# Attention scores: both single score tiles of a pair copied by VectorE and exponentiated in one instruction, a group's normalization placed ahead of P-V

## The chip, the core and the metric

The kernel runs on one core of one Trainium2 chip. A core has a matrix engine (TensorE, "PE" in the profile, with its weight loads as "PEld"), three engines for elementwise work (VectorE or "DVE", ScalarE or "ACT", GpSimd or "POOL"), and SyncE ("SP"), which here only issues transfers. Each engine works through its own queue in order; semaphores hold an instruction until what it needs is done. Matmuls write to PSUM, eight banks of 128 x 512 float32; everything else lies in SBUF or in the chip's main memory.

The metric is the device time of one execution in microseconds (us). The kernel before took 1995.16 us, the median of three runs (1995.09 to 1995.32).

## The reference

Two layers, each of them attention and a gated feed-forward block, over one sequence of S = 2048 tokens with D = 448 features, all in float32:

```python
def _A_ref(x, wq, wk, wv, wo):          # H = 16 heads, Dh = 28
    q = (x @ wq).reshape(B, S, H, Dh).transpose(0, 2, 1, 3)
    k, v = x @ wk, x @ wv               # one key and value head for all
    scores = einsum("bhqd,bkd->bhqk", q, k) * Dh ** -0.5
    o = einsum("bhqk,bkd->bhqd", softmax(scores), v)
    return o.transpose(0, 2, 1, 3).reshape(B, S, H * Dh) @ wo

def _B_ref(x, w_gate, w_up, w_down):    # F = 1792
    return (silu(x @ w_gate) * (x @ w_up)) @ w_down

x = x + _A_ref(layernorm(x)); x = x + _B_ref(layernorm(x))   # layer 0
x = x + _A_ref(layernorm(x)); x = x + _B_ref(layernorm(x))   # layer 1
```

The change is in the attention: scores, exponential, product with the values (P-V below), and the division by the sum of the exponentials.

## The kernel before

A layer runs projections (`finish`), then the score stage (`scores`), then the feed-forward block (`rest`). Float32 products outside P-V are split into a high and a low part and added up from three matmuls.

**The score stage** works by groups. A group is 512 query tokens and four heads; the list `GR` has 16 of them (4 blocks of tokens, index `c`, times 4 sets of heads, index `g`). For each group the 2048 keys pass in 16 tiles of 128. So the loop over `n` has 256 steps in a layer; `i, kt = divmod(n, NT)` gives the group and the key tile, and `d, odd = divmod(n, 2)` the pair of key tiles.

`step(n)` computes one key tile's scores for four heads: twelve matmuls (L595), three for each head, where the four heads use the four quarters of the array's rows. Heads 0 to 2 go into `three`, a PSUM tile of three banks; there are two of these, for even and odd tiles. Head 3 goes into a single bank, `one`. The single banks are number 6 and 7, by the function `single`: pair d uses bank 6 + d % 2 for its even tile and the other one for its odd tile. The exponentials go to SBUF, into `pt` (heads 0 to 2, three buffers, taken in turn from tile to tile) and `pt1` (head 3, three buffers). On ScalarE's queue a pair of tiles is four instructions: for the even tile the exponential of the single bank, straight from PSUM (L607), then that of the three banks (L608); for the odd tile that of the three banks (L602), then that of the single one (L605). For the odd tile VectorE first copies the single bank to SBUF, into `raw` (L604; one buffer), and L605 reads the copy.

`pv(d)` multiplies a pair's exponentials by the values (L638): eight matmuls with 32 columns of weights each, first the four heads of the even tile, then those of the odd one. They add up in one single bank, `single(d + 1)`: the bank that the even tile of pair d + 1 has used for its head 3. VectorE then adds the result to the group's sum in SBUF (L648; for a group's first pair it copies, L645). One column of the values is 1, so a row of the sum holds the softmax's denominator.

PE's queue, per pair d: scores of tile 2d, scores of tile 2d + 1, then `pv(d - 1)`, so that P-V is one pair behind. A group's last pair (`kt` = 14) calls `post`, whose transfers fetch the denominators (L659), and puts a function `rest` into `due` under pair d + 3. `rest` checks the denominators and inverts them on VectorE (L665 to L667), spreads them by two transfers (L669, L670), multiplies on GpSimd (L677) and splits the product. With the last group of a block of tokens, `rest` puts the block into `todo`, and `between`, at `kt` = 10, runs its output projection (48 matmuls, L578, into `three` 0 and a single bank) and adds it to the residual (L582).

Work of the next block hangs in the dictionary `later`, by the step after which it is issued: for three of the four blocks of tokens, the layer norm's statistics (L220, L221), scaling (L234) and transposes (L239), a transfer out and in, and for two of them the cut into high and low parts (`cut`, L281 to L291), all of it on VectorE but for a few small operations.

Instructions stand on each engine in the order in which the program issues them. The tile framework adds the waits: a tile that takes over a buffer waits for all readers of the tile that had it before.

Of the kernel before, what the change touches and what calls it, by code (L numbers as in the profile page):

```python
# [8 lines left out]
F32 = mybir.dt.float32  # L9
F32R = mybir.dt.float32r  # L10
AF = mybir.ActivationFunctionType
# [4 lines left out]
P = 128  # L16
# [6 lines left out]
NT = S // P  # L23
# [4 lines left out]
SCALE = DH ** -0.5  # L28
# [24 lines left out]
def forward(  # L53
# [14 lines left out]
    nc = tc.nc  # L68
# [88 lines left out]
    def weights(fc):  # L157
        fs = slice(P * fc, P * fc + P)
        r = wpool.tile([P, 4, 2, P], F32, name="wr")
        for b, src in enumerate((w_gate, w_up)):  # L160
            rows3(r[:, :, b, :], src[:, fs])
        rd = wpool.tile([P, D], F32, name="wdr")
        nc.sync.dma_start(rd, w_down[fs, :])
        h = wpool.tile([P, 4, 2, P], F32R, name="wgh", bufs=FG + 1)
        l = wpool.tile([P, 4, 2, P], F32R, name="wgl", bufs=FG + 1)
        dh = wpool.tile([P, D], F32R, name="wdh", bufs=FG + 1)
        dl = wpool.tile([P, D], F32R, name="wdl", bufs=FG + 1)
        split(h, l, r)
        split(dh, dl, rd)
        return h, l, dh, dl  # L170
# [94 lines left out]
    def cut(got, tiles, ks=range(4), copy=nc.scalar.copy):  # L265

        for k in ks:
            flipped(tiles, k, got["raw"][:, k, :], copy)
# [9 lines left out]
    def flipped(tiles, k, pt, copy):  # L278
        xh, xl, xd = tiles
        if k < 3:  # L280
            copy(xh[:, k, :], pt)  # L281
            nc.vector.tensor_tensor(xl[:, k, :], pt, xh[:, k, :], ALU.subtract)
            return
        if xd is None:
            copy(xh[:, k, :], pt)
            high = xh[64:128, k, :]
        else:
            copy(xh[0:64, k, :], pt[0:64, :])
            copy(xd[64:128, :], pt[64:128, :])
            high = xd[64:128, :]  # L290
        nc.vector.tensor_tensor(xh[64:128, k, :], pt[64:128, :], high, ALU.subtract)  # L291
# [40 lines left out]
    class Attention:  # L332
# [223 lines left out]
        def scores(self, ff):  # L556
            next(switch)
            with tc.tile_pool(name=f"at{self.layer}", bufs=1, reuse_waits="tile") as wp:
                woh = wp.tile([P, NG, D], F32R, name="woh")
                wol = wp.tile([P, NG, D], F32R, name="wol")  # L560
                on, accs, pts = {}, {}, {}
                todo, due = [], {}
                single = lambda d: banks[6 + d % 2]

                def load_wo(z):
                    r = wpool.tile([P, 4, 2, P], F32, name="wr").rearrange("p (z k) b n -> p z (k b n)", z=2)
                    nc.gpsimd.memset(r, 0.0)
                    for j in range(4):
                        nc.sync.dma_start(r[32 * j : 32 * j + DH, :, 0:D], wos[j][:, 2 * z : 2 * z + 2, :])
                    zs = slice(2 * z, 2 * z + 2)  # L570
                    split(woh[:, zs, :], wol[:, zs, :], r[:, :, 0:D])
# [14 lines left out]
                def step(n):  # L586


                    i, kt = divmod(n, NT)
                    three, one = threes[n % 2], single(n // 2 + n)  # L590
                    q, k, ks = qts[i % 2], keys[kt // 4], slice(P * (kt % 4), P * (kt % 4) + P)
                    for z, (kp, part) in enumerate(((0, 0), (1, 0), (0, 1))):
                        for j in range(4):
                            js = slice(32 * j, 32 * j + 32)
                            nc.tensor.matmul(  # L595
                                three[:, j, :] if j < 3 else one, k[js, kp, ks], q[js, part, :],
                                start=(z == 0), stop=(z == 2), tile_position=(32 * j, 0),
                            )
                    pt = wp.tile([P, 3, 512], F32, name="pt", bufs=3)
                    pt1 = wp.tile([P, 512], F32, name="pt1", bufs=3)  # L600
                    if n % 2:
                        nc.scalar.activation(pt, three, AF.Exp, scale=SCALE)  # L602
                        raw = wp.tile([P, 512], F32, name="raw")
                        nc.vector.tensor_copy(raw, one)  # L604
                        nc.scalar.activation(pt1, raw, AF.Exp, scale=SCALE)  # L605
                    else:
                        nc.scalar.activation(pt1, one, AF.Exp, scale=SCALE)  # L607
                        nc.scalar.activation(pt, three, AF.Exp, scale=SCALE)  # L608
                    pts[n] = [*(pt[:, j, :] for j in range(3)), pt1]

                def between(d):

# [18 lines left out]
                def pv(d):  # L631


                    i, kt = divmod(2 * d, NT)
                    po = single(d + 1)
                    for n in (2 * d, 2 * d + 1):
                        for j in range(4):
                            nc.tensor.matmul(  # L638
                                po[32 * j : 32 * j + 32, :], vsb[:, n % NT, :], pts[n][j],
                                start=(n == 2 * d), stop=(n > 2 * d), skip_group_check=True,  # L640
                            )
                        del pts[n]
                    if kt == 0:
                        accs[i] = halves("o2").bitcast(F32)
                        nc.vector.tensor_copy(by_tile(accs[i][:, 0, :]), in_turn(po))  # L645
                    else:
                        acc = by_tile(accs[i][:, 0, :])
                        nc.vector.tensor_tensor(acc, in_turn(po), acc, ALU.add)  # L648
                    if kt == NT - 2:
                        due[d + 3] = post(i)  # L650
# [33 lines left out]
                later = {}  # L684
                for c in range(3):
                    ff.X[c] = xtile(xpool) if c < 2 else None
                    fs, got = norm_steps(c, True)
                    n = NT * (4 * c + 5)
                    for kt, f in enumerate(fs):
                        later[n + kt] = f  # L690
                    later[n + 22] = got["load"]
                    for k in range(4) if c < 2 else ():
                        later[n + 28 + k] = lambda c=c, got=got, k=k: cut(got, ff.X[c], [k], nc.vector.tensor_copy)
                ff.norms[2] = got
                last = NT * len(GR)
                for n in range(last):
                    i, kt = divmod(n, NT)
                    if kt == 0 and i + 1 < len(GR):
                        self.parts(i + 1)
                    if kt == 3 and i + 1 < len(GR) and not full:  # L700
                        self.rows(i + 1)
                    if kt == 12 and i + 2 < len(GR):
                        self.stack(i + 2)
                    if i in (2, 3) and kt == 8:
                        load_wo(i - 2)
                    if n == NT and ff.nxt:
                        ff.nxt.below(nc.sync)
                    if kt == 8 and 10 < i <= 11 + FG:
                        ff.W[i - 11] = weights(i - 11)
                    step(n)  # L710
                    if not full and n == 1:
                        self.maxima(NC - 1, (6,))
                    if n in later:
                        later.pop(n)()
                    d, odd = divmod(n, 2)
                    if odd:
                        if d:
                            pv(d - 1)
                        between(d)
                        if d in due:  # L720
                            due.pop(d)()
                pv(last // 2 - 1)
                self.lent = None
                next(switch)
# [215 lines left out]
    fs, got = norm_steps(0)  # L940
# [27 lines left out]
    for c in range(1, NC):  # L968
        fs, got = norm_steps(c)
        n = 4 * c - 4  # L970
        at.plan[n, 1] = fs[:5]
        at.plan[n + 1, 1] = fs[5:] + [lambda c=c, got=got: at.norms.__setitem__(c, got)]
    for layer in range(2):
        at.finish()
        xb.close()
        ff = FeedForward(layer)
# [32 lines left out]
```

## Time and profile before

One profiled execution took 1994.74 us, of which the profile's span, from the first to the last instruction, is 1993.0 us.

| | |
|---|---|
| instructions | 44685 |
| VectorE busy | 816.9 us, 41% |
| ScalarE busy | 1280.6 us, 64% |
| GpSimd busy | 527.9 us, 26% |
| P-V matmuls (L638) | 4096, busy 493.3 us |
| score matmuls (L595) | 1536 into the single bank, 4608 into `three` |
| exponential of three banks (L602, L608) | 256 and 256, 1454 and 1453 ns each |
| ScalarE busy, score stage of layer 1 | nearly without a gap, four instructions in each pair |
| data moved | 77.52 MB, 39 GB/s on average |

How to read the rows below: a group's row has the line, the engine and the operation, output <- inputs with their shapes, the count, then the busy time in us, the mean of one in ns, and the engine's idle time just ahead of them with what ended it. A row of the timeline has the start and the length in us, the engine, the line, the operation, and in brackets the idle time ahead of it with the releaser. Busy time of PE is no measure of how near PE is to its limit, since records of matmuls overlap.

The row of ScalarE in the profile's 40 slices (busy tenths) shows the two score stages as the stretches with 8 or more:

```text
ACT  4899797997953333333349998979979433333332
```

### The profile page before, as it was taken

What the parts mean: (1) busy time and instruction counts of PE and PEld (TensorE: products, weight loads), DVE (VectorE), ACT (ScalarE), POOL (GpSimd) and SP (SyncE); (2) the same over time, 40 slices, a digit from 0 to 9 for tenths busy, and PEclk for the clock granted to TensorE, in tenths of its full rate; (3) what the DMA queues carried; (4) which work ended last, traced back from release to release, by engine and by line L of the source; (5) the groups of instructions that cost most, each with busy time, mean ns of one, the idle gap of its engine ahead of it and who ended that gap; (6) DMA issues with size and microseconds to landing.
All of it is one profiled execution on the core that took longest, in us unless ns stands there. A gap on an engine that the chain in (4) does not pass through costs nothing. (4 is left out here: it accounts for less than half of the span.)

```text
span 1993.0 us, 44685 instructions
## 1 busy us (share of the span) xinstructions
PE 1974.2 (99%) x18519; PEld 1326.1 (67%) x18519; DVE 816.9 (41%) x1408; ACT 1280.6 (64%) x2142; POOL 527.9 (26%) x571
## 2 busy tenths in 40 slices
PE   9999999999999999999999999999999999999998
PEld 7544545445468999999984444454454689988886
DVE  7444553544434222323554335545454432222222
ACT  4899797997953333333349998979979433333332
POOL 4212111132212233333341221111231132333320
PEclk9999999999999999999999999999999999999999
DMA  5101010121210011100130111102111101011102
GB/s 164 54 23 31 24 49 22 31 58 28 72 33 10 23 32 32 32 27 16 51 112 29 30 31 31 44 12 60 31 53 46 32 17 31 17 31 32 32 1 76
DMA packets 93382, 77.52 MB, mean 39 GB/s; under 512 B 23510, under 2 KB 76374, under 8 KB 93174
## 3 DMA queue, kind: packets, MB, share of 16 engines
q1 hardware_dynamic: 92758, 74.36, 13.5%
q8 instruction: 146, 2.39, 0.5%
q14 instruction: 62, 0.51, 0.1%
q10 hardware_dynamic: 416, 0.26, 0.0%
HBM read 55.06 MB, written 18.74 MB: 37 GB/s over the span
## 5 line engine op out<-in xcount | busy, mean ns | idle before, releaser
L638 PE MATMUL bank<-pt,vsb 128*32 128x512 f32 x4096 | 493.3, 598 | 0.5
L595 PE MATMUL bank<-qstack,keys 32*128 32x512 f32 x1536 | 484.6, 425 | 2.6 <-DVE xres L582 1.7
L595 PE MATMUL three<-qstack,keys 32*128 32x512 f32 x4608 | 463.7, 426 | 3.2 <-DVE vt L531 2.9
L595 PEld LDWEIGHTS three<-qstack,keys 32*128 32x128 f32 x4608 | 254.7, 183 | 296.9 <-ACT pt L608 178.6
L321 PE MATMUL bank<-xh,wgh 64*128 64x512 f32 x1728 | 436.2, 389 | 0.1
L602 ACT ACTIVATE pt<-three 128x1536 f32<-128x1536 f32 x256 | 372.2, 1454 | 3.5 <-PE bank L638 2.8
L608 ACT ACTIVATE pt<-three 128x1536 f32<-128x1536 f32 x256 | 372.0, 1453 | 0.0
L321 PE MATMUL bank<-xh,wgl 64*128 64x512 f32 x1404 | 362.1, 390 | 0.0
L321 PE MATMUL bank<-wdh,h 64*128 64x448 f32 x1792 | 329.8, 364 | 1.4 <-ACT h L869 1.0
L321 PE MATMUL bank<-xl,wgh 64*128 64x512 f32 x1296 | 327.3, 389 | 0.0
L868 DVE TENSOR_TENSOR sg<-bank,sg 128x512 f32<-128x512 f32 x112 | 77.5, 692 | 497.6 <-ACT sg L867 488.5
L638 PEld LDWEIGHTS bank<-pt,vsb 128*32 128x32 f32 x4096 | 107.1, 109 | 250.2 <-issue 154.4
L604 DVE COPY raw<-bank 128x512 f32<-128x512 f32 x256 | 177.4, 693 | 227.6 <-PE bank L595 226.0
L321 PEld LDWEIGHTS bank<-xh,wgh 64*128 64x128 f32 x1728 | 256.4, 184 | 16.5 <-issue 0.9
L786 POOL TENSOR_TENSOR xres<-stage,xres 128x448 f32<-128x448 f32 x108 | 127.7, 1205 | 499.2 <-ACT stage L785 499.2
L648 DVE TENSOR_TENSOR o<-bank,o 128x512 f32<-128x512 f32 x224 | 154.9, 692 | 239.6 <-PE bank L638 234.3
L321 PEld LDWEIGHTS bank<-wdh,h 64*128 64x128 f32 x1792 | 240.2, 184 | 15.5 <-issue 2.0
L595 PEld LDWEIGHTS bank<-qstack,keys 32*128 32x128 f32 x1536 | 244.4, 183 | 7.8 <-DVE xres L582 3.6
L328 ACT COPY seen<-bank 128x1 f32<-128x1 f32 x664 | 81.0, 163 | 238.7 <-PE bank L321 235.9
L321 PEld LDWEIGHTS bank<-xh,wgl 64*128 64x128 f32 x1404 | 211.7, 184 | 14.0
L321 PE MATMUL bank<-wdl,h 64*128 64x448 f32 x896 | 214.9, 367 | 0.0
L867 ACT ACTIVATE sg<-bank 128x512 f32<-128x512 f32 x112 | 67.3, 601 | 223.2 <-PE bank L321 214.3
(128 smaller groups left out, 2266.7 us busy)
## 6 DMA issues: line engine op xcount, KB each, us to landing
o<-rd SPq DMA_DIRECT2D x32, 256.0 KB
qd<-stage SPq DMA_DIRECT2D x32, 224.0 KB
qraw<-qd SPq DMA_DIRECT2D x128, 56.0 KB
xt<-xn SPq DMA_DIRECT2D x28, 224.0 KB
wdr<-in_B_w_down_dram SPq DMA_DIRECT2D x28, 224.0 KB
xn<-xt SPq DMA_DIRECT2D x7, 768.0 KB
wr<-in_B_w_gate_dram SPq DMA_DIRECT2D x28, 192.0 KB
wr<-in_B_w_up_dram SPq DMA_DIRECT2D x28, 192.0 KB
```

The source lines that it names most:

```text
L321: nc.tensor.matmul(po, a, b, start=start, stop=stop, skip_group_check=True)
L328: nc.scalar.copy(seen[:, i : i + 1], po[:, 0:1])
L595: nc.tensor.matmul(three[:, j, :] if j < 3 else one, k[js, kp, ks], q[js, part, :], start=(z == 0), stop=(z == 2), tile_position=(32 * j, 0),)
L602: nc.scalar.activation(pt, three, AF.Exp, scale=SCALE)
L604: nc.vector.tensor_copy(raw, one)
L608: nc.scalar.activation(pt, three, AF.Exp, scale=SCALE)
L638: nc.tensor.matmul(po[32 * j : 32 * j + 32, :], vsb[:, n % NT, :], pts[n][j], start=(n == 2 * d), stop=(n > 2 * d), skip_group_check=True,)
L648: nc.vector.tensor_tensor(acc, in_turn(po), acc, ALU.add)
L786: nc.gpsimd.tensor_tensor(r, s, r, ALU.add)
L867: nc.scalar.activation(by_tile(sg), in_turn(pg[0]), AF.Silu)
L868: nc.vector.tensor_tensor(by_tile(sg), in_turn(pg[1]), by_tile(sg), ALU.mult)
```

## The change

The single bank of the even tile is no longer read by ScalarE. VectorE copies the single bank of both tiles of a pair into the two halves of one tile `raw`, and after the second copy ScalarE takes the exponential of both halves in one instruction of 1024 columns, into a `pt1` of two halves (two buffers instead of three). `raw` still has one buffer, of double size. The exponentials of the three banks now come first for both tiles.

A group's `rest` is issued ahead of `pv(d - 1)` and its sum, not behind them and `between`. The layer norm's steps start one step of the loop later and come at every second step instead of every step; its transfer in and its cut move along.

```diff
@@ scores, step
                     pt = wp.tile([P, 3, 512], F32, name="pt", bufs=3)
-                    pt1 = wp.tile([P, 512], F32, name="pt1", bufs=3)
+                    nc.scalar.activation(pt, three, AF.Exp, scale=SCALE)
+                    if n % 2 == 0:
+                        copied["raw"] = wp.tile([P, 2, 512], F32, name="raw")
+                        copied["pt"] = wp.tile([P, 2, 512], F32, name="pt1", bufs=2)
+                    nc.vector.tensor_copy(copied["raw"][:, n % 2, :], one)
+                    pts[n] = [*(pt[:, j, :] for j in range(3)), copied["pt"][:, n % 2, :]]
                     if n % 2:
-                        nc.scalar.activation(pt, three, AF.Exp, scale=SCALE)
-                        raw = wp.tile([P, 512], F32, name="raw")
-                        nc.vector.tensor_copy(raw, one)
-                        nc.scalar.activation(pt1, raw, AF.Exp, scale=SCALE)
-                    else:
-                        nc.scalar.activation(pt1, one, AF.Exp, scale=SCALE)
-                        nc.scalar.activation(pt, three, AF.Exp, scale=SCALE)
-                    pts[n] = [*(pt[:, j, :] for j in range(3)), pt1]
+                        nc.scalar.activation(copied["pt"], copied["raw"], AF.Exp, scale=SCALE)
@@ scores, the steps of the layer norm
-                    n = NT * (4 * c + 5)
+                    n = NT * (4 * c + 5) + 1
                     for kt, f in enumerate(fs):
-                        later[n + kt] = f
-                    later[n + 22] = got["load"]
+                        later[n + 2 * kt] = f
+                    later[n + 2 * len(fs) + 6] = got["load"]
                     for k in range(4) if c < 2 else ():
-                        later[n + 28 + k] = lambda c=c, got=got, k=k: cut(got, ff.X[c], [k], nc.vector.tensor_copy)
+                        later[n + 2 * len(fs) + 14 + 2 * k] = lambda c=c, got=got, k=k: cut(got, ff.X[c], [k], nc.vector.tensor_copy)
@@ scores, the loop over n
                     if odd:
+                        if d in due:
+                            due.pop(d)()
                         if d:
                             pv(d - 1)
                         between(d)
-                        if d in due:
-                            due.pop(d)()
```

Where instructions stand on the engines now, with what each one waits for (the engine whose semaphore it is; numbers behind names tell buffers' uses apart). ScalarE's queue, two pairs early in layer 0, before:

```order
L607 ACTIVATE pt1_875<-bank7_79 128x512 [waits PE_49]
L608 ACTIVATE pt_874<-three0_800 128x1536
L602 ACTIVATE pt_891<-three1_801 128x1536 [waits PE_49,Activation_49]
L605 ACTIVATE pt1_892<-raw_894 128x512 [waits DVE_49,PE_49]
L607 ACTIVATE pt1_920<-bank6_78 128x512 [waits PE_49,Activation_49]
```

The same place now, where L600 is the exponential of three banks, of the even and then of the odd tile, and L607 that of the two copies:

```order
L600 ACTIVATE pt_873<-three0_800 128x1536 [waits PE_49]
L600 ACTIVATE pt_891<-three1_801 128x1536 [waits PE_49,Activation_49]
L607 ACTIVATE pt1_876<-raw_875 128x1024 [waits DVE_49]
L600 ACTIVATE pt_917<-three0_800 128x1536 [waits PE_49,Activation_49]
L600 ACTIVATE pt_934<-three1_801 128x1536 [waits PE_49,Activation_49]
```

Four instructions of a pair have become three; the odd tile's exponential of three banks still waits for PE, the even tile's single bank has moved to the end of the pair, and its wait is for VectorE.

VectorE's queue at the same place, before (L604 is the copy of the odd tile's single bank, L645 and L648 take P-V's result):

```order
L604 COPY raw_894<-bank6_78 128x512 [waits PE_49,Activation_49]
L645 COPY o2_905<-bank7_79 128x512 [waits PE_49,Activation_49]
L604 COPY raw_938<-bank7_79 128x512 [waits PE_49,Activation_49]
L648 TENSOR_TENSOR o2_905<-bank6_78,o2_905 128x512 [waits DVE_49,PE_49,Activation_49]
L604 COPY raw_981<-bank6_78 128x512 [waits PE_49,Activation_49]
```

And now, with the same line number for both copies of a pair (L643 and L646 take P-V's result):

```order
L604 COPY raw_875<-bank7_79 128x512 [waits PE_49,Activation_49]
L604 COPY raw_875<-bank6_78 128x512 [waits PE_49]
L643 COPY o2_903<-bank7_79 128x512 [waits PE_49]
L604 COPY raw_919<-bank6_78 128x512 [waits PE_49,Activation_49]
L604 COPY raw_919<-bank7_79 128x512 [waits PE_49]
L646 TENSOR_TENSOR o2_903<-bank6_78,o2_903 128x512 [waits DVE_49,PE_49]
```

There are two copies a pair in place of one, and the first of them, that of the even tile, waits for ScalarE: it takes over the one buffer of `raw`.

PE's queue at P-V of the first pair's successor, before:

```order
L638 MATMUL bank6_78<-pt_874,vsb_94 32x512 [waits Activation_49]
L638 MATMUL bank6_78<-pt_874,vsb_94 32x512 x2
L638 MATMUL bank6_78<-pt1_875,vsb_94 32x512
L638 MATMUL bank6_78<-pt_891,vsb_94 32x512 x3
L638 MATMUL bank6_78<-pt1_892,vsb_94 32x512
```

And now:

```order
L636 MATMUL bank6_78<-pt_873,vsb_94 32x512 [waits DVE_49]
L636 MATMUL bank6_78<-pt_873,vsb_94 32x512 x2
L636 MATMUL bank6_78<-pt1_876,vsb_94 32x512 [waits Activation_49]
L636 MATMUL bank6_78<-pt_891,vsb_94 32x512 x3
L636 MATMUL bank6_78<-pt1_876,vsb_94 32x512
```

P-V's first matmul, which takes over the bank of an even tile, waited for ScalarE and now waits for VectorE; the fourth, which reads the fused exponential, has a wait of its own.

More of the change, by code (lines that the diff above doesn't have):

```diff
@@ L561, in scores @@
                 on, accs, pts = {}, {}, {}
-                todo, due = [], {}
+                todo, due, copied = [], {}, {}
                 single = lambda d: banks[6 + d % 2]
```

## The prediction, made before the changed kernel ran

> **What bounds the kernel now.** I read the page's busy times first, then the list of waits, then the timeline of a few pairs of key tiles inside the score loop of the second layer.
>
> ```profile
> PE 1974.2 (99%) x18519; PEld 1326.1 (67%) x18519; DVE 816.9 (41%) x1408; ACT 1280.6 (64%) x2142; POOL 527.9 (26%) x571
> ...
> L602 ACT ACTIVATE pt<-three 128x1536 f32<-128x1536 f32 x256 | 372.2, 1454 | 3.5 <-PE bank L638 2.8
> ```
>
> Over the whole span PE looks like the bound (99%). But matmul records overlap, and the share says nothing of the score loop, which holds 256 pairs of key tiles (L602 runs once a pair: x256, both layers). There the list of waits (engine and line that waited, releaser, us in total, times, longest) has PE waiting for ScalarE in nearly every pair:
>
> ```profile
> PEld bank L638 <- ACT pt L607: 92.8, 249, 0.6
> ...
> ACT pt L607 <- PE bank L595: 65.1, 7, 10.7
> ...
> ACT pt L602 <- PE bank L638: 2.8, 7, 0.7
> ```
>
> ScalarE's L607 waits 7 times only. P-V (L638) waits for L607 249 times, because L607 empties the single bank that P-V writes next. One steady pair (start, length, engine, line):
>
> ```profile
> 1103.56 0.59 ACT L607 ACTIVATE pt<-bank 128x512 f32<-128x512 f32 x1
> ...
> 1104.04 1.45 ACT L608 ACTIVATE pt<-three 128x1536 f32<-128x1536 f32 x1
> ...
> 1104.20 1.92 PE L638 MATMUL bank<-pt,vsb 128*32 128x512 f32 x16
> ...
> 1105.38 1.45 ACT L602 ACTIVATE pt<-three 128x1536 f32<-128x1536 f32 x1
> ...
> 1106.06 0.51 PE L595 MATMUL three<-qstack,keys 32*128 32x512 f32 x3
> ...
> 1106.25 0.69 DVE L648 TENSOR_TENSOR o<-bank,o 128x512 f32<-128x512 f32 x1 [1.19 <-PE bank L638]
> ...
> 1106.73 0.62 ACT L605 ACTIVATE pt<-raw 128x512 f32<-128x512 f32 x1
> ...
> 1106.88 0.50 PE L595 MATMUL three<-qstack,keys 32*128 32x512 f32 x3
> ...
> 1107.25 0.59 ACT L607 ACTIVATE pt<-bank 128x512 f32<-128x512 f32 x1
> ```
>
> From L607 to the next L607 a pair takes 1107.25 - 1103.56 = **3.69 us**. ScalarE has no gap: L607 to L608 0.48, to L602 1.34, to L605 1.35, to L607 0.52. There is also a loop through three engines, with the same sum: L607 starts, ends, and P-V starts 0.64 later (0.59 and 0.05); L602 starts 1.18 after P-V; L605 1.35 after that; the next L607 0.52 after that: 0.64 + 1.18 + 1.35 + 0.52 = 3.69. Why L602 hangs on P-V is in the code: `pt` has three buffers, so tile 2d+1 writes the buffer of tile 2d-2, which the first half of P-V of pair d-1 still reads. Whether the loop is real shows where P-V comes late:
>
> ```profile
> 1266.51 1.46 ACT L608 ACTIVATE pt<-three 128x1536 f32<-128x1536 f32 x1
> ...
> 1267.51 1.92 PE L638 MATMUL bank<-pt,vsb 128*32 128x512 f32 x16
> ...
> 1268.68 1.45 ACT L602 ACTIVATE pt<-three 128x1536 f32<-128x1536 f32 x1 [0.71 <-PE bank L638]
> ```
>
> L602 starts 2.17 after L608 instead of 1.34, but again 1.17 after P-V. So ScalarE's own load and this loop bound the stage together, with no slack between them. PE needs less: P-V to the first scores 1.86 (1104.20 to 1106.06), to the second scores 0.82, and about as much again, some 3.48.
>
> **The change part by part.** Durations of the instructions concerned (line, engine, count, busy us, mean ns):
>
> ```profile
> L602 ACT ACTIVATE pt<-three 128x1536 f32<-128x1536 f32 x256 | 372.2, 1454 | 3.5 <-PE bank L638 2.8 <-ACT pt L608 0.3
> ...
> L604 DVE COPY raw<-bank 128x512 f32<-128x512 f32 x256 | 177.4, 693 | 227.6 <-PE bank L595 226.0 <-ACT pt L607 1.4
> L605 ACT ACTIVATE pt<-raw 128x512 f32<-128x512 f32 x256 | 159.2, 622 | 0.0
> ...
> L607 ACT ACTIVATE pt<-bank 128x512 f32<-128x512 f32 x256 | 151.4, 591 | 65.3 <-PE bank L595 65.1
> ```
>
> *One exponential of 1024 columns in place of L607 and L605.* No row has this form. The slope is (1454 - 591) / 1024 = 0.843 ns a column, so 622 + 512 x 0.843 = 1.05 us. From below: 1454 - 512 x 0.843 = 1.02, the price of reading PSUM; from above: 0.62 and a whole further step of 0.52, 1.14. I take 1.05, since L605 is the row with the same source. On ScalarE's queue it takes 1.05 less the 0.10 by which L605 and L607 overlap, 0.95, instead of 0.48 + 0.52: ScalarE's own load falls from 3.69 to **3.64**. That is all that the fusion can save: 0.05 x 256 = 13 us. By the Trainium skill's page "ScalarE: Activation LUTs", section "What ACT_TABLE_LOAD costs", an instruction more costs a fixed 186 ns, of which 93 overlap, so that 24 us would be the estimate; the case in which it comes out is a rival below.
>
> *One copy more per pair, and where it stands.* VectorE is 41% busy and gets 256 x 0.69 us more; its load per pair becomes 3 x 0.69 = 2.08 of 3.69. What costs is the wait: `raw` has one buffer of two halves, so the copy of tile 2d waits for the fused exponential of pair d-1, which ends last on ScalarE. P-V of pair d-1 writes the bank that this copy empties. Before, the bank was emptied by L607, which followed L605 on its own engine by 0.52. The copy itself then sits at the head of VectorE's queue, with the second copy and the sum behind it. The two handovers are short:
>
> ```profile
> 701.30 0.60 ACT L867 ACTIVATE sg<-bank 128x512 f32<-128x512 f32 x1 [1.91 <-PE bank L321]
> ...
> 701.93 0.69 DVE L868 TENSOR_TENSOR sg<-bank,sg 128x512 f32<-128x512 f32 x1 [4.68 <-ACT sg L867]
> ...
> 1201.22 0.62 DVE L582 TENSOR_TENSOR xres<-bank,xres 128x448 f32<-128x448 f32 x1 [0.68 <-PE bank L578]
> ...
> 1201.89 0.18 PEld L595 LDWEIGHTS bank<-qstack,keys 32*128 32x128 f32 x1 [0.60 <-DVE xres L582]
> ```
>
> ScalarE to VectorE 0.03 (701.90 to 701.93), VectorE to PE 0.05 (1201.84 to 1201.89).
>
> **The new loop**, from the end of one fused exponential to the end of the next: 0.03 + copy 0.69 + 0.05, P-V starts; + 1.18, the exponential of tile 2d+1 may start (the `pt` buffers are unchanged); + 1.35, the fused one starts; + 1.05, it ends. Sum **4.35 us a pair**, 0.66 more than 3.69. Everything else fits inside: PE's 3.48; the exponential of tile 2d (1.35) runs while the copy and P-V do (1.95); the sum, 2.05 after P-V starts (1104.20 to 1106.25) and 0.69 long, ends at 0.77 + 2.74 = 3.51, 0.87 before the next copy is due.
>
> *The group's normalization and sums ahead of P-V, the layer norm's steps spread to every second tile.* They are VectorE's:
>
> ```profile
> L282 DVE TENSOR_TENSOR xl<-xn,xh 128x512 fp32r<-128x512 f32 x21 | 14.0, 689 | 0.5
> ...
> L666 DVE TENSOR_TENSOR fine<-fine,under 128x16 f32<-128x16 f32 x64 | 11.2, 175 | 2.2
> L665 DVE TENSOR_SCALAR under<-rs 128x16 f32<-128x16 f32 x64 | 10.9, 170 | 1.1
> ...
> L281 DVE CAST xh<-xn 128x512 fp32r<-128x512 f32 x12 | 8.0, 669 | 0.7 <-DMA xn<-xt 0.7
> ...
> L667 DVE RECIPROCAL rs<-rs 128x16 f32<-128x16 f32 x32 | 7.8, 245 | 0.0
> ```
>
> The group's steps now stand ahead of a sum: 2 x 0.17 + 2 x 0.175 + 0.245 = 0.94; a cut is 0.67 + 0.69 = 1.36. Between the second copy (ends at 1.41) and the sum (may start at 2.82) VectorE has 1.41 free, and 0.87 more before a delayed sum delays the copy: cost nothing in this loop. Without that cover each would add up to its own length, 32 x 0.94 = 30 us. The SP transfers and GpSimd products that follow the reciprocal move along by a part of a pair and are needed three pairs later (`kt` 10). Two layer-norm steps in one pair delayed P-V in the row at 1267.51; spread out they no longer do: of L602's idle time I take the whole 3.5 us as gained.
>
> **The sum.** In each layer three pairs contain an output projection, which breaks the loop:
>
> ```profile
> L578 PE MATMUL three<-woh,onh 128*128 128x448 f32 x72 | 27.0, 375 | 0.0
> ```
>
> (72 = 12 for each of 6.) There PE is what everything waits for, and L607's 0.59 + 0.05 between scores and P-V becomes a copy's 0.69 + 0.05: 0.1 each, 0.6 in all. 2 x 127 steps from pair to pair less 6 are 248: 248 x 0.66 = 163.7. The last fused exponential of a layer is 0.43 longer than L605: 0.9. So 163.7 - 3.5 + 0.6 + 0.9 = 162 us. The profiled execution took 1994.74 us (span 1993.0 and 1.74 around it; the median of the runs is 0.42 above): 1994.7 + 162 = **2156 us**. With the fused exponential at 1.02, 2148; at 1.14, 2178.
>
> **Rivals.** (1) *The copy doesn't hold P-V* and ScalarE alone bounds: 3.64 a pair, 1994.7 - 13 = **1982**, the other side. It decides if the exponential of pair d-1 were over before the scores of pair d; against it speaks that ScalarE is the engine without a gap and that `raw` is single. By the Trainium skill's fixed cost for an instruction, an estimate of 24 us, this case would end at 1971; the steps of 0.48 and 0.52 in the rows give about half of that. (2) *L602's wait falls away* (P-V's first half done in time): then the loop goes over two pairs: 0.77 to P-V, 1.86 to the scores, 1.04 from there to their exponential (1201.89 above to L607 here), 1.34 + 1.35 + 1.05:
>
> ```profile
> 1202.93 0.60 ACT L607 ACTIVATE pt<-bank 128x512 f32<-128x512 f32 x1 [10.63 <-PE bank L595]
> ```
>
> that is 7.41, 3.71 a pair: +0.02 x 248 = 5, **2000**. The row at 1268.68 speaks against it. (3) *The clock gate.* PE will pause some 4.35 - 3.48 = 0.87 in one piece in every pair. This trace has a pause that cost clock:
>
> ```profile
> 1051.03 0.50 PE L595 MATMUL three<-qstack,keys 32*128 32x512 f32 x3 [1.81 <-DVE vt L531]
> ```
>
> The stretch behind it (its length, PE's busy time, instructions, granted clock) and the page's row of the clock:
>
> ```profile
> 1052.00:1054.00 2.00, 2.00 (x9) 0.50 0.00 0
> ```
>
> ```profile
> PEclk9999999999999999999999999999999999999999
> ```
>
> At half clock PE's 3.48 become 6.96; with one pair in four so, 0.25 x (6.96 - 4.35) x 248 = 162 more, **2318**. Against it speaks that PE already lacks work for 3.69 - 3.48 = 0.21 of each pair, and the page has 9 tenths or more in every slice. The Trainium skill's page "TensorE: Matmul & The Clock Gate", section "A second HAM failure mode: psum-queue depth-cycling", tells of short pauses between groups of matmuls that made the clock swing, which speaks for this case; this trace shows it for the pause of 1.81 and for no shorter one.
>
> **How the numbers follow.** Forecast 0.87, (1) 0.05, (2) 0.04, (3) 0.04. A difference of under 0.2% (4 us) can't be told from none. (1) is faster; of (2), whose 5 us lie at that edge, half counts as same; the rest is slower: 0.05, 0.02, 0.93. The range takes the cost ends 2148 and 2178, below them 20 pairs that escape the loop (13 us), above them stalls twice as large as L602's present 3.5: 2135 to 2185. The three rivals lie outside, 0.13 together.
>
> **What would show it.** Right: pairs 4.35 apart; on ScalarE a gap of about 0.6 ahead of the second 1536-column exponential, put down to P-V; the first copy of a pair starting 0.03 after the fused exponential ends, and P-V 0.05 after the copy; the fused one near 1.05; clock unchanged. Wrong: a copy that starts well before the fused exponential ends, (1); no gap on ScalarE but P-V late, (2); P-V's matmuls at twice 598 ns, (3).

## The result, and the profile after

| | before | after |
|---|---|---|
| time, median | 1995.12 us (4 runs) | 2170.6 us (4 runs, 2168.82 to 2171.6) |
| span of the profiled execution | 1993.0 us | 2169.0 us |
| ratio, with its 95% interval | | 1.0877 [1.0864, 1.0891] |

The changed kernel is slower by 8.8%. Predicted were 2156 us, 14.6 less than measured, in a range of 2135 to 2185.

The page of the changed kernel: first the busy times (busy us, share of the span, count), then the groups of the score stage. L600 is now the exponential of three banks for both tiles, L607 the fused one, L604 both copies, L636 is P-V.

```profile
PE 1983.3 (91%) x18519; PEld 1313.1 (61%) x18519; DVE 977.6 (45%) x1664; ACT 1289.6 (59%) x1886; POOL 528.0 (24%) x571
...
L600 ACT ACTIVATE pt<-three 128x1536 f32<-128x1536 f32 x512 | 740.8, 1447 | 235.2 <-PE bank L636 174.0
L636 PE MATMUL bank<-pt,vsb 128*32 128x512 f32 x4096 | 496.8, 601 | 156.3 <-DVE raw L604 153.6
...
L604 DVE COPY raw<-bank 128x512 f32<-128x512 f32 x512 | 330.7, 686 | 228.1 <-ACT pt L607 216.7
L607 ACT ACTIVATE pt<-raw 128x1024 f32<-128x1024 f32 x256 | 268.6, 1049 | 0.0
```

ScalarE's busy time has hardly moved, from 1280.6 to 1289.6 us, although it runs 256 instructions fewer. What is new is idle time: 235 us of ScalarE ahead of L600, which had 3.5 ahead of L602, and 156 of PE ahead of P-V. The list of waits names the ring (who waited, for whom, total us, times, longest):

```profile
PEld bank L636 <- DVE raw L604: 264.3, 252, 1.7
...
DVE raw L604 <- ACT pt L607: 216.7, 242, 1.2
...
ACT pt L600 <- PE bank L636: 174.0, 254, 7.9
...
DVE sg L234 <- POOL rstd L226: 16.5, 6, 7.5
```

P-V waits for the copy, the copy for the fused exponential, and the odd tile's exponential, which precedes the fused one, for P-V: three waits of some 250 times each, so each binds once a pair. (Before, P-V waited 92.8 us for ScalarE.) The last row, six waits only, comes up again below. One steady pair of the changed kernel's timeline (start, length, engine, line; idle time ahead in brackets):

```profile
1169.73 1.05 ACT L607 ACTIVATE pt<-raw 128x1024 f32<-128x1024 f32 x1
...
1170.68 1.44 ACT L600 ACTIVATE pt<-three 128x1536 f32<-128x1536 f32 x1
...
1170.82 1.29 DVE L604 COPY raw<-bank 128x512 f32<-128x512 f32 x2 [0.92 <-ACT pt L607]
...
1171.56 1.92 PE L636 MATMUL bank<-pt,vsb 128*32 128x512 f32 x16 [0.66 <-DVE raw L604]
...
1172.74 1.45 ACT L600 ACTIVATE pt<-three 128x1536 f32<-128x1536 f32 x1 [0.62 <-PE bank L636]
...
1174.09 1.05 ACT L607 ACTIVATE pt<-raw 128x1024 f32<-128x1024 f32 x1
```

Read it as a ring: the fused exponential ends at 1170.78, the copy starts at 1170.82, P-V 0.74 later, the odd tile's exponential 1.18 after P-V, the fused one 1.35 after that. 1174.09 - 1169.73 = 4.36 us; predicted were 4.35.

In 248 pairs at 0.66 us more, that accounts for 164 of the 175 us. Two stalls, one in each layer, hold some 15 more; all the rest gives about 4 back, mostly in pairs that were longer than 3.69 before and now take 4.35 like the others. The second layer's, in the timeline of the changed kernel:

```profile
1647.41 1.04 POOL L139 TENSOR_SCALAR wgh<-wr 128x1024 fp32r<-128x1024 f32 x1 [1.71 <-DMA wr<-in_B_w_up_dram]
...
1648.54 2.36 POOL L140 TENSOR_TENSOR wgl<-wr,wgh 128x1024 fp32r<-128x1024 f32 x1
...
1651.52 1.13 POOL L140 TENSOR_TENSOR wdl<-wdr,wdh 128x448 fp32r<-128x448 f32 x1
...
1653.01 1.01 POOL L226 TENSOR_TENSOR rstd<-rstd,halfn 128x4 f32<-128x4 f32 x1
1654.06 0.51 DVE L234 TENSOR_SCALAR sg<-xres,mv,rstd 128x448 f32<-128x448 f32 x1 [7.42 <-POOL rstd L226]
...
1654.49 0.68 DVE L646 TENSOR_TENSOR o<-bank,o 128x512 f32<-128x512 f32 x1
...
1655.23 0.79 PE L595 MATMUL bank<-qstack,keys 32*128 32x512 f32 x1 [5.94 <-DVE o L646]
...
1656.80 2.86 PE L636 MATMUL bank<-pt,vsb 128*32 128x512 f32 x16
...
1658.84 1.45 ACT L600 ACTIVATE pt<-three 128x1536 f32<-128x1536 f32 x1 [7.83 <-PE bank L636]
```

The layer norm's reciprocal deviation, `rstd`, is worked out on GpSimd (L225, L226). It now stands behind the cut of the feed-forward weights (L139, L140): GpSimd first waits 1.71 us for their transfer (`DMA wr`), then works on the cut for some 5 us. VectorE's scaling (L234) waits 7.42 us for `rstd` at the head of its queue. The sum of P-V's result (L646) stands behind the scaling, and PE's next scores, which take over the bank that the sum reads, wait 5.94 us for it; P-V comes behind these scores. From one odd tile's exponential to the next this pair takes 11.57 us, 7.2 more than the others, with some 0.9 in it because P-V itself took 2.86 in place of 1.92. The first layer's takes 11.62, and the pair behind it 0.9 more than the others.

### The profile page after: what moved, and what is told of

Its sections match the earlier page's. It is cut to its first block, busy times and chain, and to the rows that moved or that the text cites. A ratio compares the mean times of both kernels' runs of the same rounds, so it can differ in the third digit from the quotient of the medians.

```text
span 2169.0 us, 44376 instructions
## 1 busy us (share of the span) xinstructions
PE 1983.3 (91%) x18519; PEld 1313.1 (61%) x18519; DVE 977.6 (45%) x1664; ACT 1289.6 (59%) x1886; POOL 528.0 (24%) x571
## 5 line engine op out<-in xcount | busy, mean ns | idle before, releaser
L600 ACT ACTIVATE pt<-three 128x1536 f32<-128x1536 f32 x512 | 740.8, 1447 | 235.2 <-PE bank L636 174.0
L636 PE MATMUL bank<-pt,vsb 128*32 128x512 f32 x4096 | 496.8, 601 | 156.3 <-DVE raw L604 153.6
L595 PE MATMUL bank<-qstack,keys 32*128 32x512 f32 x1536 | 474.4, 426 | 14.5 <-DVE o L646 12.6
L604 DVE COPY raw<-bank 128x512 f32<-128x512 f32 x512 | 330.7, 686 | 228.1 <-ACT pt L607 216.7
L636 PEld LDWEIGHTS bank<-pt,vsb 128*32 128x32 f32 x4096 | 107.6, 109 | 425.0 <-DVE raw L604 264.3
L607 ACT ACTIVATE pt<-raw 128x1024 f32<-128x1024 f32 x256 | 268.6, 1049 | 0.0
L646 DVE TENSOR_TENSOR o<-bank,o 128x512 f32<-128x512 f32 x224 | 154.0, 687 | 233.6 <-PE bank L636 233.2
L675 POOL TENSOR_TENSOR o<-o 128x512 f32<-128x512 f32 x32 | 41.0, 1281 | 714.0 <-DMA o<-rd 481.3
```

The lines of the kernel that those rows point to most:

```text
L595: nc.tensor.matmul(three[:, j, :] if j < 3 else one, k[js, kp, ks], q[js, part, :], start=(z == 0), stop=(z == 2), tile_position=(32 * j, 0),)
L604: nc.vector.tensor_copy(copied["raw"][:, n % 2, :], one)
L607: nc.scalar.activation(copied["pt"], copied["raw"], AF.Exp, scale=SCALE)
L636: nc.tensor.matmul(po[32 * j : 32 * j + 32, :], vsb[:, n % NT, :], pts[n][j], start=(n == 2 * d), stop=(n > 2 * d), skip_group_check=True,)
```

## The experiments

Each expectation was written before its kernel ran; "before" in them is the kernel before on the same chip. Times are medians, with the ratio to that kernel and its interval.

**1. A second buffer for `raw`.** The edit takes the ring apart (and makes room by a single `pt1`):

```diff
-  copied["raw"] = wp.tile([P, 2, 512], F32, name="raw")
-  copied["pt"] = wp.tile([P, 2, 512], F32, name="pt1", bufs=2)
+  copied["raw"] = wp.tile([P, 2, 512], F32, name="raw", bufs=2)
+  copied["pt"] = wp.tile([P, 2, 512], F32, name="pt1", bufs=1)
```

> The changed kernel with two buffers of raw in place of one, and one buffer of the fused pt1 in place of two, so that the memory stays the same. All 512 copies remain. Theory (the loop: fused exponential, copy, P-V, odd tile's exponential): the even tile's copy no longer waits for the fused exponential of the pair before; the loop shortens to 0.05 + 1.18 + 1.35 + 1.05 = 3.63 us, ScalarE's own load of 3.64 bounds, and 248 x (4.35 - 3.64) = 176 us go: about 1995 us. Rival (the added copies cost their own length, 256 x 0.69 = 177 us, which is the whole loss): the copies are all there, so about 2171 us.

2040.32 us, 1.0222 [1.0206, 1.0237]. The timeline of one pair of this kernel:

```profile
1110.33 1.92 PE L636 MATMUL bank<-pt,vsb 128*32 128x512 f32 x16
...
1112.18 0.50 PE L595 MATMUL three<-qstack,keys 32*128 32x512 f32 x3
...
1113.30 1.46 DVE L604 COPY raw<-bank 128x512 f32<-128x512 f32 x2 [0.29 <-PE bank L595]
...
1114.04 1.92 PE L636 MATMUL bank<-pt,vsb 128*32 128x512 f32 x16
```

The copy no longer waits for the fused exponential, and 130 of the 175 us are gone, not the 176 of the theory: the single buffer is the cause of most of the loss, not the number of copies. But pairs are 1114.04 - 1110.33 = 3.71 us apart, not shorter than before. **A third ring** holds them there: P-V, 1.85 to the even tile's scores, 1.12 until the copy of their bank starts, 0.69 of copy, 0.05, P-V. Scores to P-V's bank took 0.64 by way of ScalarE before (0.59 and 0.05); a copy by VectorE takes 0.74. Of the other 45 us this ring holds some 8 (0.03 in each of 254 pairs); the rest is in stalled pairs. The largest wait of VectorE there, in this kernel's list of waits:

```profile
DVE sg L234 <- POOL rstd L226: 28.0, 6, 9.2
```

**2. P-V reads the odd tile first.** This was to move the release of the buffer that the odd tile's exponential waits for:

```diff
-  for n in (2 * d, 2 * d + 1):
+  for n in (2 * d + 1, 2 * d):
...
-    start=(n == 2 * d), stop=(n > 2 * d), skip_group_check=True,
+    start=(n > 2 * d), stop=(n == 2 * d), skip_group_check=True,
```

> The changed kernel, with P-V taking the odd tile of a pair first and the even tile second. The exponential of the next odd tile then waits for the second half of P-V, 0.86 us later. Theory: P-V's first half is a part of the loop, so a pair takes 4.35 + 0.86 = 5.21 us and the kernel 2171 + 248 x 0.86 = about 2384 us. Rival (only the copies count, or only the way from the fused exponential to P-V): the same work in another order, about 2171 us.

2173.19 us, 1.0888 [1.0868, 1.0908]: no change, and not the 2384 of the theory. In this kernel's timeline the exponential still starts 1.17 after P-V:

```profile
1171.23 1.92 PE L636 MATMUL bank<-pt,vsb 128*32 128x512 f32 x16 [0.65 <-DVE raw L604]
...
1172.40 1.45 ACT L600 ACTIVATE pt<-three 128x1536 f32<-128x1536 f32 x1 [0.62 <-PE bank L636]
```

Either the wait was not for P-V's first half, or the tile takes whichever of the three `pt` buffers is released first in the program, so that the odd tile's turn changes with the order. The next kernel on this tells these apart.

**3. Both tiles' buffers released in P-V's second half.**

```diff
-  for n in (2 * d, 2 * d + 1):
+  for half in range(2):
       for j in range(4):
+          n = 2 * d + (half ^ (j == 2))
...
-              start=(n == 2 * d), stop=(n > 2 * d), skip_group_check=True,
+              start=(half == 0), stop=(half == 1), skip_group_check=True,
```

> The changed kernel, with P-V's eight matmuls in an order (three heads of the even tile and one of the odd tile, then the others) in which neither tile's exponentials are read to the end before its second half. Theory: the odd tile's exponential takes whichever buffer of pt P-V releases first, so that taking the odd tile first changed nothing; now the first release comes 0.86 us later, a pair takes 4.35 + 0.86 = 5.21 us and the kernel about 2171 + 240 x 0.86 = 2377 us. Rival (the exponential does not wait for P-V's release at all, and the 1.18 us between the two have another cause): about 2171 us.

2373.36 us, 1.1893 [1.1867, 1.1919], as expected. From this kernel's timeline:

```profile
1292.20 1.92 PE L637 MATMUL bank<-pt,vsb 128*32 128x512 f32 x16 [0.70 <-DVE raw L604]
...
1294.22 1.45 ACT L600 ACTIVATE pt<-three 128x1536 f32<-128x1536 f32 x1 [1.46 <-PE bank L637]
...
1297.39 1.07 PE L637 MATMUL bank<-pt,vsb 128*32 128x512 f32 x8 [0.70 <-DVE raw L604]
```

The exponential starts 2.02 after P-V instead of 1.18, and the pair takes 1297.39 - 1292.20 = 5.19 instead of 4.35: the same 0.84. So the link from P-V to the odd tile's exponential is a `pt` buffer, released when P-V has read it, and it lies on the ring.

**4. The layer norm's steps at their old places.** All else is as in the changed kernel:

```diff
-  n = NT * (4 * c + 5) + 1
+  n = NT * (4 * c + 5)
   for kt, f in enumerate(fs):
-      later[n + 2 * kt] = f
-  later[n + 2 * len(fs) + 6] = got["load"]
+      later[n + kt] = f
+  later[n + 22] = got["load"]
...
-      later[n + 2 * len(fs) + 14 + 2 * k] = ...
+      later[n + 28 + k] = ...
```

> The changed kernel with the layer norm's steps where they were before (from the group's first step on, one per step). In the changed kernel two pairs, one in each layer, take 11.6 us, where the scaling waits 7.4 us for rstd, which stands on GpSimd's queue behind the splits of feed-forward weights. Theory: before, rstd stood ahead of those splits, so both stalls go and 14.5 us with them: about 2156 us. Rival (the spread hides more than that, since two VectorE steps in a pair delay the sum and the copy): at least as many us come back elsewhere, 2171 us or more.

2164.15 us, 1.0847 [1.0827, 1.0867]. Between the two. The two long waits for `rstd` are gone, but four pairs that now hold two cut steps each take 5.69 to 5.70 us instead of 4.35. Two steps alone are not the reason: the pair ahead of each of the four holds two as well and takes 4.35. In the four, one of the two steps runs beside GpSimd and takes twice as long. In this kernel's timeline, one of VectorE's, then GpSimd's:

```profile
317.02 1.65 DVE L282 TENSOR_TENSOR xl<-xn,xh 128x512 fp32r<-128x512 f32 x1
```

```profile
316.79 1.32 POOL L140 TENSOR_TENSOR qstack<-qraw,qstack 128x512 fp32r<-128x512 f32 x1
```

The subtraction (L282) takes 0.69 in the pair ahead. The spread did help here, and lost more at `rstd`.

**5. The spread kept, only the steps up to `rstd` earlier.** These go in one after another, from step 80 of the loop on (and likewise in the other blocks); the rest stays spread:

```diff
-  later[n + 2 * kt] = f
+  later[n - 1 + kt if kt < 5 else n + 2 * kt] = f
```

> The changed kernel, with only the layer norm's statistics and rstd issued at consecutive steps as before the change (so that rstd stands ahead of the group's GpSimd product and of the weights' splits); scaling, transposes and cuts stay at every second step. Theory: the two pairs of 11.6 us go, nothing comes back, 2 x (7.3 + 0.5) = about 16 us less: 2155 us. Rival (the stall comes from the transposes or from SP's transfers): 2171 us.

2155.91 us, 1.0809 [1.079, 1.0828]. The group of L234 in the changed kernel, and then in this one:

```profile
L234 DVE TENSOR_SCALAR sg<-xres,mv,rstd 128x448 f32<-128x448 f32 x28 | 17.6, 628 | 16.7 <-POOL rstd L226 16.5
```

```profile
L234 DVE TENSOR_SCALAR sg<-xres,mv,rstd 128x448 f32<-128x448 f32 x28 | 17.7, 634 | 0.2
```

The wait goes from 16.5 us to nothing, and the time falls by 14.7 to the 2156 of the prediction: this wait is what the prediction's sum left out.

**6. Is the third ring real? Half of the even tile's copy.** With two buffers of `raw`, the even tile's copy takes 256 columns of 512; the other half of that tile's head 3 is left out, its scores standing at zero.

```diff
+  raws = [wp.tile([P, 2, 512], F32, name=f"raw{i}") for i in range(2)]
+  for r in raws:
+      nc.gpsimd.memset(r, 0.0)
...
-  copied["raw"] = wp.tile([P, 2, 512], F32, name="raw")
+  copied["raw"] = raws[n // 2 % 2]
...
-  nc.vector.tensor_copy(copied["raw"][:, n % 2, :], one)
+  w = 512 if n % 2 else 256
+  nc.vector.tensor_copy(copied["raw"][:, n % 2, 0:w], one[:, 0:w])
```

(`pt1` has one buffer, as in the first experiment.)

> As the run with two buffers of raw (2040 us, pairs 3.72 us apart), but the copy of the even tile's single bank takes 256 of its 512 columns; the other half of those scores is left out (zeros), all other instructions are the same. Theory (a third loop: P-V, scores of the even tile, copy of their single bank, P-V, 1.85 + 1.12 + 0.69 + 0.05 = 3.71 us): with some 0.39 us for the copy it takes 3.41, ScalarE's 3.64 bounds, and 235 x 0.075 = 18 us go: about 2022 us. Rival (ScalarE bounds already and is slowed to 3.72 by something else): the pairs stay at 3.72, 2040 us.

2044.37 us, 1.0248 [1.0231, 1.0265]: by its time, a miss. The pairs are as the theory has them, in this kernel's timeline:

```profile
1120.16 0.42 DVE L608 COPY raw<-bank 128x256 f32<-128x256 f32 x1 [0.29 <-PE three L598]
...
1120.81 1.93 PE L640 MATMUL bank<-pt,vsb 128*32 128x512 f32 x16
...
1124.44 1.92 PE L640 MATMUL bank<-pt,vsb 128*32 128x512 f32 x16
```

A copy shorter by 0.27 makes the pair 3.63 instead of 3.72. It shortens by 0.09 only, because ScalarE's own load binds next (its rows follow each other there without a gap), and that is the 3.64 of the prediction's first rival. The time was lost at the start of each layer's stage, where the zeroing stands on GpSimd's queue behind other work and the first copy waits for it:

```profile
77.02 1.02 DVE L608 COPY raw<-bank 128x256 f32<-128x256 f32 x2 [10.90 <-POOL raw L565]
```

Twice some 11 us; without them it would be about 2022, as expected. That last number is a subtraction, not a run.

**7. Two buffers for `raw`, and `rstd` earlier.** The first experiment, with all steps of the layer norm two steps earlier (`n = NT * (4 * c + 5) - 1`).

> As the run with two buffers of raw, and the layer norm's steps still at every second step but two steps earlier, so that rstd stands ahead of the splits of the feed-forward weights on GpSimd's queue. Theory: both losses go; ScalarE alone bounds with 3.64 us a pair, 0.05 under the kernel before: about 1981 us, faster than both kernels. Rival for the stalls (they come from the transfer of the weights, not from the order on GpSimd): 1995 us. Rival for the loop (copies cost their length): 2156 us.

2055.12 us, 1.0291 [1.0276, 1.0305]: slower than the first, a miss. `rstd` is now ahead of the weights' cut, but behind the group's product on GpSimd, which waits for the transfer of the denominators. This kernel's list of waits, and then GpSimd's timeline:

```profile
DVE sg L234 <- POOL rstd L226: 36.4, 6, 6.5
```

```profile
282.94 1.29 POOL L675 TENSOR_TENSOR o<-o 128x512 f32<-128x512 f32 x1 [20.01 <-DMA o<-rd]
```

All six blocks stall by some 6 us. GpSimd's queue holds the product there, behind a wait of 20 us for a transfer, and in the third block of a layer the weights' cut with its 5 us of work; a step that VectorE needs soon must be ahead of both.

**8. Two buffers for `raw`, and everything else where it stood before.** The first experiment with the old places of the layer norm's steps (as in 4) and of a group's `rest`.

> Two buffers of raw and one of pt1, with the layer norm's steps and the group's normalization where they were before the change: what is left is the fused exponential and the added copy alone, without the wait on raw. Theory (third loop): pairs at 3.72 us, 0.03 more than before, 248 x 0.03 = 7 us, and some us where two VectorE steps in a pair delay the copies: about 2005 us, still slower than the kernel before. Rival (ScalarE's shorter work shows once the stalls are gone): 1982 us.

2024.58 us, 1.0146 [1.0127, 1.0165]. The best of the kernels with two copies, and still slower than before. Two P-V of a pair's distance in this kernel's timeline:

```profile
1122.80 1.92 PE L636 MATMUL bank<-pt,vsb 128*32 128x512 f32 x16
...
1126.52 1.92 PE L636 MATMUL bank<-pt,vsb 128*32 128x512 f32 x16
```

3.72 us, as expected. Against the 2005 that were expected, about 13 us come from the 30 pairs with a group's normalization, nearly all of them 0.43 longer: VectorE's copy now stands in the ring. Most of the rest is in pairs with a cut step, some of them 1.3 to 2.75 longer. The place of the normalization seems to matter here: in the first experiment, where it stands ahead of P-V and its sum, 16 of these 30 pairs take 3.72. Two buffers with that place and the early `rstd` of experiment 5 together were not run.

**9 to 11. The parts of the change that move instructions, each in the kernel before.** The spread as the change has it; the spread with `rstd` early (as in 5); a group's `rest` ahead of P-V.

```diff
 # the spread
-  n = NT * (4 * c + 5)
+  n = NT * (4 * c + 5) + 1
-      later[n + kt] = f
+      later[n + 2 * kt] = f
...
 # a group's rest
+  if d in due:
+      due.pop(d)()
   if d:
       pv(d - 1)
   between(d)
-  if d in due:
-      due.pop(d)()
```

> The kernel before, with the change's new places of the layer norm's steps alone. Theory: rstd waits on GpSimd's queue behind the splits of the weights as in the changed kernel, two stalls of 7.3 us or, since pairs are shorter here and the same transfer takes the same time, somewhat more (9.7 as with two buffers of raw), less the 4 us that the spread gains: 2005 to 2012 us. Rival (the stall belongs to the fused exponential's queue): 1991 us.

2046.88 us, 1.0262 [1.0246, 1.0278]: the right direction, three to five times the size. This kernel's list of waits, and then GpSimd's timeline in the first block:

```profile
DVE sg L234 <- POOL rstd L226: 37.7, 6, 9.9
```

```profile
243.94 1.29 POOL L677 TENSOR_TENSOR o<-o 128x512 f32<-128x512 f32 x1 [20.32 <-DMA o<-rd]
```

All six blocks wait here, not two: with the shorter pairs, `rstd` comes behind the group's product, as in experiment 7, and in the third block of a layer behind the weights' cut as well. These waits add up to 38 us of the 52 that are lost; the rest was not taken apart.

> The kernel before, with the layer norm's scaling, transposes and cuts at every second step, but statistics and rstd at consecutive steps as they were. Theory: the pairs of the kernel before in which two VectorE steps delay P-V (by 0.2 to 0.8 us each, some 4 us in all) go, and nothing comes back: about 1991 us, at the edge of what can be told from no change. Rival (GpSimd or the transfers take it back): 1995 us or more.

2001.15 us, 1.0029 [1.0017, 1.0041]: the rival was right. With the waits for `rstd` gone, cut steps now run beside GpSimd's instructions, the longest of them beside its cut of the weights. In this kernel's timeline VectorE, and then GpSimd:

```profile
437.63 0.42 DVE L281 CAST xh<-xn 128x512 fp32r<-128x512 f32 x1
...
441.39 1.14 DVE L281 CAST xh<-xn 128x512 fp32r<-128x512 f32 x1
442.56 2.74 DVE L282 TENSOR_TENSOR xl<-xn,xh 128x512 fp32r<-128x512 f32 x1
...
447.02 0.69 DVE L604 COPY raw<-bank 128x512 f32<-128x512 f32 x1 [1.12 <-PE bank L595]
```

```profile
441.20 1.04 POOL L139 TENSOR_SCALAR wgh<-wr 128x1024 fp32r<-128x1024 f32 x1 [0.98 <-DMA wr<-in_B_w_up_dram]
442.33 2.42 POOL L140 TENSOR_TENSOR wgl<-wr,wgh 128x1024 fp32r<-128x1024 f32 x1
```

The cut takes 1.14 and 2.74 us in place of 0.42 and 0.69, and each of its two parts ends a little after GpSimd's instruction that started ahead of it (at 442.53 after 442.24; at 445.30 after 444.75).

> The kernel before, with the group's normalization and sums issued ahead of P-V, the third part of the change alone. Theory: its 0.94 us of VectorE's queue now stand ahead of the sum instead of ahead of the odd tile's copy; both have room here (the copy ends 1.3 us before its exponential starts): within 4 us of the kernel before, 1992 to 1999 us. Rival (the sum's bank holds up the scores that follow, 30 groups by up to 0.4 us): 2007 us.

1994.92 us (10 runs), 0.9999 [0.999, 1.0008]: it costs nothing there, as expected.

No kernel ran faster than the one before by more than the noise, and the rows say why none with two whole copies a pair did: with `raw` doubled the third ring holds a pair at 3.72 us, above the 3.69 of before.

## Why the prediction was right, and where it was off

- **What bounds the kernel before: right.** Two limits of 3.69 with no slack between them meant that a link made longer would show in full, and it did.
- **The fused exponential, 1.05: right** (1.049).
- **The new ring, 4.35: right,** each link within 0.01: 0.03 to the copy, 0.69 of copy, 0.05 to P-V, 1.18 to the odd tile's exponential, 1.35, 1.05. Doubling `raw` (experiment 1) opens it, lengthening the link through `pt` by 0.84 lengthens the pair by as much (experiment 3).
- **Why the odd tile's exponential waits for P-V: right in the wait, wrong in the detail.** The prediction took the three buffers to go round in turn, so that it would be the buffer of tile 2d-2 whatever P-V's order. Turning P-V's order around changed nothing, so the buffer is not fixed by turn. That the tile framework hands out the buffer that comes free first would explain both kernels, and by it the buffer of tile 2d-2 would still be the one in the changed kernel; this was inferred from the times and not looked at.
- **The normalization ahead of P-V, nothing: right as far as it was tried,** 0.9999 in the kernel before (experiment 11). Inside the changed kernel it was not tried alone, but there 29 of the 30 pairs that hold a group's normalization take 4.35 us, like the rest.
- **The layer norm's steps "spread out", from which the prediction took 3.5 us as gained: this term was mis-sized, in sign too.** It looked at VectorE's work in those steps and not at the queue that the spread moves one of them past: `rstd` on GpSimd slid behind the weights' cut, some 5 us of GpSimd's work behind a wait for a transfer. That cost 14.7 us (experiment 5 without it), which is the distance between 2170.6 and 2156. In the changed kernel the spread as a whole costs 6.5 us against the old places (experiment 4), where 3.5 were to be gained. GpSimd's cut of the weights stood in the timeline of before as well (at 1453.21, for 5.3 us).
- **Rival 1, ScalarE alone, 1982: could not have come out,** even without the ring of `raw`. The third ring, which the prediction did not see, holds the pair at 3.72; only with half a copy left out did a pair reach 3.63. By that row the fusion saves 0.06 a pair, 15 us in all. The Trainium skill's fixed cost for an instruction, on the page "ScalarE: Activation LUTs", section "What ACT_TABLE_LOAD costs", made that an estimate of 24; the measured pair is nearer to the 13 from the steps.
- **Rival 2, the ring over two pairs, 2000: did not happen** in the changed kernel. The odd tile's exponential waited for P-V 254 times there, 174.0 us in all. That its 3.71 a pair is close to the third ring's 3.72 is chance: they are different rings.
- **Rival 3, the clock: did not happen.** PE pauses 0.66 us ahead of P-V in every pair, and the page's row of the granted clock has 9 tenths or more throughout; the mean is 0.995. The exception, behind the stall, is in the last section.

## What to carry to other kernels

A copy that frees a bank early is worth nothing if the copy's own target has one buffer: before handing work to another engine, follow the ring through every buffer that the new instruction takes over, and add the links up; here that gave the pair to 0.01 us. When a step is moved, list every engine on which it issues something, small operations too, and what stands ahead of it on that queue in the new place, work as well as waits for transfers: one operation of 1 us on GpSimd cost 7 us twice. And when a ring is opened, work out the next one before expecting the gain: here it was slightly longer than the old kernel's pair.

## What the runs showed of the hardware

**VectorE against GpSimd.** Beside a GpSimd cut of 2.42 us, VectorE's subtraction of two SBUF operands took 2.74 us instead of 0.69 (the rows of experiment 9), and the copy from SBUF to SBUF 1.14 instead of 0.42. The Trainium skill's page "SBUF — State Buffer", section "SBUF: two separate sides", states that the two engines share a pair of ports that one of them holds for a whole instruction while the other blocks, where VectorE reads two SBUF operands or copies in its fast mode. The rows agree: each of VectorE's two instructions ends shortly after GpSimd's. The same subtraction with one operand in PSUM is not touched, in that run (times: shortest, median, longest in ns):

```profile
L282 DVE TENSOR_TENSOR xl<-bank,xh x27: 672/680/693, 12.1 to 1619.5; 128x512 fp32r<-128x512 f32 x27
```

None of the 27 is longer than 0.69, though 17 of them run beside instructions of GpSimd. The prediction did not weigh the shared ports: its 0.67 us for the cast (L281) is a mean over casts from 0.42 to 1.53 us, and the 1.53, at 1262.05 in the timeline of before, stands in VectorE's work ahead of the late P-V at 1267.51 on which the term for the spread rests.

**The clock behind a pause.** The windows of the changed kernel (from and to, length in us, PE's busy time and instructions, granted clock, DMA), one in a steady stretch and then three around the stall shown above:

```profile
1170.00:1175.00 5.00, 4.34 (x56) 1.00 0.00 0
```

```profile
1648.00:1654.00 6.00, 1.28 (x19) 0.83 0.00 0
1654.00:1658.00 4.00, 2.77 (x17) 0.50 0.00 0
1658.00:1662.00 4.00, 3.45 (x36) 0.91 0.00 0
```

PE stood still for 5.94 us, up to 1655.23. The granted clock fell to half within this pause (the first window's mean is 0.83) and was back in the third window; in between P-V took 2.86 instead of 1.92 us. In the first layer a pause of 6.00 us did the same, and P-V took 3.64. Pauses of 0.66 us in every pair of 4.35 left it at 1.00. The section on the Trainium skill's page "TensorE: Matmul & The Clock Gate" that the prediction weighed, by which short pauses between groups of matmuls make the clock swing, is not borne out for pauses of this length and rate.
